# A linear recurrence feeding a soft mixture of experts: channel pairing, a fixed engine order, later weight loads and fewer exps

## The chip, the cores and the metric

The kernel runs on one core of a Trainium2 chip. The metric is the device time in microseconds (us) of one execution; where several executions were timed, I give the median. A core has TensorE (PE in the profile; PEld is its weight load), VectorE (DVE), ScalarE (ACT), GpSimd (POOL) and a queue engine (SP); data moves between memory and core by 16 DMA engines.

## The reference

Two stages. First, a gated recurrence along a sequence of 5056 tokens, for 4 batches and 256 channels. Then a soft mixture of 8 experts with 4 slots each over all 20224 tokens: a softmax over the tokens dispatches them to the slots, and a softmax over the 32 slots combines the answers.

```
sig = 1 / (1 + exp(-f_logit));  f = lb + (1 - lb) * sig;  i = 1 - f
for t in range(S):
    h = f[:, t] * h + i[:, t] * x[:, t]        # y[:, t] = h
logits = y @ phi                                # [20224, 32]
d = softmax over tokens(logits);  slot_input = d.T @ y
slot_out[e] = relu(slot_input[e] @ w1[e]) @ w2[e]
out = softmax over slots(logits) @ slot_out     # [20224, 256]
```

## The kernel before

The work is cut in *units*: 512 tokens of one batch (the last group has 448). There are 10 groups of 4 batches, so 40 units. A unit goes through these steps; this is the source, with cuts marked:

```python
W_FROM = 22            # a weight load at each of the units 22 to 37, as written
        def gate(n):
            n_p = rows(n // B)
            su = sup.tile([P, R, D, 2], BF16, name="su", tag="su")
            sus[n] = su
            nc.scalar.activation(su[:n_p, :, :, 1], fs.pop(n)[:n_p], ACT.Sigmoid,
                                 scale=-1.0)
            nc.gpsimd.tensor_tensor(su[:n_p, :, :, 0], su[:n_p, :, :, 1],
                                    xs.pop(n)[:n_p], ALU.mult)

        def to_channels(n):
            n_p = rows(n // B)
            su = sus.pop(n)
            for dc in range(DC):
                ps = psu.tile([P, P, R], F32, name="ps", tag="ps")
                for r in range(R):
                    nc.tensor.transpose(
                        ps[:, :n_p, r],
                        su[:n_p, r, ds(dc * P, P)].bitcast(F32).rearrange("p c o -> p (c o)"),
                        ident_f[:n_p, :n_p])
                pss[n, dc] = ps

        def scan(n):
            T = rows(n // B) * R
            h = hpool.tile([P, G, DC], BF16, name="h", tag="h")
            hs[n] = h
            for dc in range(DC):
                ps = pss.pop((n, dc)).rearrange("c p r -> c (p r)").bitcast(BF16)
                ps = ps.rearrange("c (t o) -> c t o", o=2)
                a = apool.tile([P, G], F32, name="a", tag="a")
                nc.scalar.activation(a[:, :T], ps[:, :T, 1], ACT.Identity,
                                     scale=nomlb[:, ds(dc, 1)], bias=1.0)
                nc.vector.tensor_tensor_scan(
                    h[:, :T, dc], a[:, :T], ps[:, :T, 0],
                    hs[n - B][:, ds(G - 1, 1), dc] if n >= B else 0.0,
                    ALU.mult, ALU.add)
        # ... to_tokens(n): 4 transposes of h back to tokens into hp, then a copy by DVE into ht
        # ... logits(g): 8 matmuls with phi for a group of 4 units, then exp by ACT into etall
        # ... weights_to_tokens(g): 4 transposes of etall into ep, copy into et, row sums into rsum (DVE)
        # ... slots(g): 16 matmuls, ht by et, summed over all tokens into slot_ps

        for n in range(n_unit + 8):
            if n + AHEAD < n_unit:
                load(n + AHEAD)
            if n + 2 < n_unit:
                gate(n + 2)
            if W_FROM <= n < W_FROM + 2 * E:
                load_w(n - W_FROM)
            if n + 1 < n_unit:
                to_channels(n + 1)
            if n < n_unit:
                scan(n)
            m = n - 1
            if 0 <= m < n_unit:
                to_tokens(m)
                if m % B == B - 1:
                    logits(m // B)
            m = n - 2
            if m >= 0 and m % B == B - 1 and m < n_unit:
                weights_to_tokens(m // B)
            m = n - 3
            if m >= 0 and m % B == B - 1 and m < n_unit:
                slots(m // B)
```

So ACT makes 1-sigmoid, POOL multiplies it with x, and both values of one channel lie side by side as two bf16 in one 32-bit word. PE transposes such words (as if they were f32) to channel-major, ACT turns one half into the decay `a` and DVE scans. **The order of instructions on an engine is not the order above**: a scheduler in the framework reorders them, and the trace shows in what order they ran.

After the recurrence comes a *middle* (normalisation and experts, mostly PE) and an *output* stage (a matmul per tile, scaling, and a store of 20.7 MB). The change leaves both as they are.

The softmax here doesn't subtract the row's maximum and nothing guards it: scores larger than these inputs give would overflow.

Of the kernel before, what the change touches and what calls it, by code (L numbers as in the profile page):

```python
# [18 lines left out]
def kernel(  # L19
# [19 lines left out]
    R = 4  # L39
# [10 lines left out]
    make_identity(nc, ident_f)  # L50
    ident = consts.tile([P, P], BF16, name="ident")
    nc.vector.tensor_copy(ident, ident_f)
# [9 lines left out]
    with nc.allow_non_contiguous_dma(reason="256 words"):  # L62
        nc.sync.dma_start(out=lb, in_=lower_bound.rearrange("(dc p) -> p dc", p=P))
# [5 lines left out]
    nc.sync.dma_start(out=phi_f, in_=moe_phi.rearrange("(dc p) s -> p dc s", p=P))  # L69
    phi = consts.tile([P, DC, NS], BF16, name="phi")  # L70
    for dc in range(DC):
        nc.vector.tensor_scalar_mul(phi[:, dc], phi_f[:, dc], omlb[:, ds(dc, 1)])
# [7 lines left out]
    csum = store.tile([P, n_grp], F32, name="csum")  # L80
    slot_sb = store.tile([P, D], F32, name="slot_sb")
    w1_r = moe_w1.rearrange("e (dc p) f -> e p dc f", p=P)
# [10 lines left out]
    W_FROM = 22  # L93

    with tc.tile_pool(name="ld", bufs=7) as ld, \
# [3 lines left out]
         tc.tile_pool(name="htok", bufs=2) as htok, \  # L99
         tc.tile_pool(name="etok", bufs=2) as etok, \  # L100
         tc.tile_pool(name="psu", bufs=4, space=PSUM) as psu, \
         tc.tile_pool(name="ptp", bufs=2, space=PSUM) as ptp, \
# [4 lines left out]
        xs, fs, sus, pss, hs, hps, hts, lgs, ets, eps = ({} for _ in range(10))  # L107
# [14 lines left out]
        def gate(n):  # L122
            n_p = rows(n // B)
            su = sup.tile([P, R, D, 2], BF16, name="su", tag="su")
            sus[n] = su
            nc.scalar.activation(su[:n_p, :, :, 1], fs.pop(n)[:n_p], ACT.Sigmoid,  # L126
                                 scale=-1.0)
            nc.gpsimd.tensor_tensor(su[:n_p, :, :, 0], su[:n_p, :, :, 1],  # L128
                                    xs.pop(n)[:n_p], ALU.mult)

        def to_channels(n):
            n_p = rows(n // B)
            su = sus.pop(n)
            for dc in range(DC):
                ps = psu.tile([P, P, R], F32, name="ps", tag="ps")
                for r in range(R):
                    nc.tensor.transpose(  # L137
                        ps[:, :n_p, r],
                        su[:n_p, r, ds(dc * P, P)].bitcast(F32).rearrange("p c o -> p (c o)"),
                        ident_f[:n_p, :n_p])  # L140
                pss[n, dc] = ps

        def scan(n):
            T = rows(n // B) * R
            h = hpool.tile([P, G, DC], BF16, name="h", tag="h")
            hs[n] = h
            for dc in range(DC):
                ps = pss.pop((n, dc)).rearrange("c p r -> c (p r)").bitcast(BF16)
                ps = ps.rearrange("c (t o) -> c t o", o=2)
                a = apool.tile([P, G], F32, name="a", tag="a")  # L150
                nc.scalar.activation(a[:, :T], ps[:, :T, 1], ACT.Identity,  # L151
                                     scale=nomlb[:, ds(dc, 1)], bias=1.0)
                nc.vector.tensor_tensor_scan(  # L153
                    h[:, :T, dc], a[:, :T], ps[:, :T, 0],
                    hs[n - B][:, ds(G - 1, 1), dc] if n >= B else 0.0,
                    ALU.mult, ALU.add)

        def to_tokens(n):
# [6 lines left out]
            if b == 0:  # L165
                hts[g] = htok.tile([P, B, R, D], BF16, name="ht", tag="ht")
            nc.vector.tensor_copy(  # L167
                hts[g][:n_p, b].rearrange("p r d -> p (r d)").bitcast(F32),
                hp[:n_p].rearrange("p r c -> p (r c)"))

        def logits(g):
            T = rows(g) * R
            lg = plg.tile([P, G], F32, name="lg", tag="lg")
            for dc in range(DC):
                for b in range(B):
                    nc.tensor.matmul(lg[ds(b * NS, NS), :T], phi[:, dc],  # L176
                                     hs[g * B + b][:, :T, dc],
                                     start=dc == 0, stop=dc == DC - 1,
                                     skip_group_check=True)
            nc.scalar.activation(etall[:, ds(g * G, T)], lg[:, :T], ACT.Exp,  # L180
                                 accum_out=csum[:, ds(g, 1)])
# [24 lines left out]
        AHEAD = 6  # L206
        for n in range(AHEAD):
            load(n)
        gate(0)
        gate(1)  # L210
        to_channels(0)
        for n in range(n_unit + 8):
            if n + AHEAD < n_unit:
                load(n + AHEAD)
            if n + 2 < n_unit:
                gate(n + 2)
            if W_FROM <= n < W_FROM + 2 * E:
                load_w(n - W_FROM)
            if n + 1 < n_unit:
                to_channels(n + 1)  # L220
            if n < n_unit:
                scan(n)
            m = n - 1
            if 0 <= m < n_unit:
                to_tokens(m)
                if m % B == B - 1:
                    logits(m // B)
            m = n - 2
            if m >= 0 and m % B == B - 1 and m < n_unit:
                weights_to_tokens(m // B)  # L230
# [112 lines left out]
```

## Time and profile before

The median is 277.25 us of 3 runs (277.19 to 278.37). The profiled execution spans 276.7 us.

| stretch of the profile (us) | what happens | us |
|---|---|---|
| 0 to 11.7 | first tokens land, first scan starts | 11.7 |
| 11.7 to 87.7 | units 0 to 12 are scanned | 76.0, 5.8 a unit |
| 87.7 to 193.7 | units 13 to 39 | 106.0, 3.9 a unit |
| 193.7 to 218.3 | middle | 24.6 |
| 218.3 to 276.7 | output | 58.4 |

From the page of the kernel before: the DVE row and the two DMA rows, for 40 equal slices of 6.9 us (a digit is tenths of busy time; GB/s is what was moved).

```profile
DVE  2386477365423959779596797958600375556450
DMA  6999999999999999978686840000000099999996
GB/s 184 415 309 300 305 301 304 301 276 278 277 278 391 410 410 409 397 261 286 219 322 195 260 135 0 0 0 2 0 2 0 2 383 405 404 405 405 403 381 213
```

The DMA engines are full in slices 2 to 17, yet move only some 300 GB/s in slices 3 to 12, while DVE is half idle. The missing bandwidth has a name in the timeline of POOL and in the list of DMA issues (last column: us from issue to landing). Two of the 16 weight loads, the first and the last, and the landing of the last:

```profile
9.68 0.89 POOL L89 DMA_DIRECT2D w_sb_90<-in_moe_w_dram  x1
55.49 0.59 POOL L91 DMA_DIRECT2D w_sb_105<-in_moe_w_dram  x1 [0.31 <-DMA w_sb_97<-in_moe_w_dram]
w_sb_105<-in_moe_w_dram POOLq DMA_DIRECT2D x1, 512.0 KB, 30.0
```

The source puts them at units 22 to 37; the scheduler has moved them up, and they share the DMA engines with the tokens until 85.5 us (55.5 + 30.0). They read 32-bit words and write bf16, so each counts 0.5 MB moved for 1 MB read (256 x 1024 words of 4 bytes), which is why "full" looks like 300 GB/s: 8.39 MB of weights in 76 us are 110 GB/s, and 301 + 110 is about the 410 of the slices without weights (an estimate). Their first use is at 199.5 us.

The table of stretches (busy us of each engine with its number of instructions, granted PE clock, DMA share, GB/s):

```profile
11.70:87.70 76.00, 43.51 (x250) 30.50 (x250) 42.46 (x46) 43.83 (x53) 41.68 (x30) 0.73 1.06 301
103.90:169.50 65.60, 45.26 (x312) 32.65 (x304) 52.25 (x57) 52.30 (x65) 37.49 (x17) 0.83 0.75 261
```

In the second stretch 16 units pass, 4.1 us each, with DMA to spare. DVE (third number, 52.25) and ACT (52.30) are busy 80% each: neither is full. The list of waits of the whole profile, cut to seven rows, says what waits for what (engine, its work, what released it: us in total, times, longest):

```profile
PE ps L137 <- POOL su L128: 52.1, 27, 9.8
POOL su L128 <- ACT su L126: 46.9, 21, 3.9
POOL su L128 <- DMA x_t<-in_x_dram: 32.2, 8, 5.9
DVE h L153 <- ACT a L151: 30.3, 14, 7.1
DVE ht L167 <- PE hp L164: 30.2, 16, 4.9
ACT a L151 <- PE ps L137: 29.5, 24, 4.9
ACT su L126 <- DMA f_t<-in_f_logit_dram: 24.2, 8, 4.6
```

The two DMA rows belong to the first stretch and the start before it (all but 2.8 us). The others form a ring: DVE waits for the decay, the decay for the transposes, those for POOL's product, that for the sigmoid. But the two stretches differ. DVE waits 26.4 of its 30.3 us for the decay in the first; between 103.9 and 169.5 us alone, the same list gives 28.2 us for POOL's wait for the sigmoid, 17.0 for PE's wait for the product, 11.0 for ACT's wait for the transposes, but for DVE only 1.3 us for the decay and 10.6 us for `hp`, the transposes of h back to tokens. In mid-recurrence DVE's idle time is 13.4 of 65.6 us. Last, three groups of instructions (count, busy us, mean ns, then idle time before them):

```profile
L128 POOL TENSOR_TENSOR su<-su,x_t 128x1024 bf16<-128x1024 bf16 x36 | 84.6, 2356 | 75.8 <-ACT su L126 39.7 <-DMA x_t<-in_x_dram 32.2 <-ACT a L151 2.6
L126 ACT ACTIVATE su<-f_t 128x1024 bf16<-128x1024 f32 x36 | 48.2, 1358 | 24.3 <-DMA f_t<-in_f_logit_dram 24.2
L126 ACT ACT_TABLE_LOAD x10 | 12.8, 1283 | 5.0 <-DMA f_t<-in_f_logit_dram 4.2 <-PEq L327 0.7
```

### The profile page before, as it was taken

To read this page: it belongs to the slowest core of one execution; us is meant where nothing else is said; L and a number is where in the kernel's file an instruction comes from. 1 tells how busy PE (TensorE), PEld (TensorE's weight loads), DVE (VectorE), ACT (ScalarE), POOL (GpSimd) and SP (SyncE) were. 2 spreads that over 40 slices of the span, in tenths; PEclk is the share of its full clock that TensorE was granted. 3 is DMA by queue.
4 is the path that set the end of the run, shared out by engine and by line. 5 is a ranking of instruction groups with operands and counts; after the bars stand their busy time and mean duration, and the time that the engine had idled before them with its cause. 6 is when DMAs were issued, how large, how long until landed. Compare 5 with 4: busy or idle time off the path is not lost. (4 is left out here: it accounts for less than half of the span.)

```text
span 276.7 us, 3255 instructions
## 1 busy us (share of the span) xinstructions
PE 175.5 (63%) x1118; PEld 119.2 (43%) x1118; DVE 163.4 (59%) x180; ACT 159.3 (58%) x232; POOL 111.9 (40%) x64
## 2 busy tenths in 40 slices
PE   0475755644564969566775866739599797677620
PEld 0344543423342746454553644526497532223310
DVE  2386477365423959779596797958600375556450
ACT  3577576553635596886869777795020255445440
POOL 1979746642225357365555746459300000000000
PEclk9999768765566666899798597995755955555555
DMA  6999999999999999978686840000000099999996
GB/s 184 415 309 300 305 301 304 301 276 278 277 278 391 410 410 409 397 261 286 219 322 195 260 135 0 0 0 2 0 2 0 2 383 405 404 405 405 403 381 213
DMA packets 20977, 70.77 MB, mean 256 GB/s; under 512 B 2720, under 2 KB 2720, under 8 KB 20960
## 3 DMA queue, kind: packets, MB, share of 16 engines
q1 hardware_dynamic: 17632, 62.17, 60.0%
q0 software_dynamic: 3328, 8.39, 15.5%
q8 instruction: 9, 0.15, 0.2%
q14 instruction: 8, 0.07, 0.1%
HBM read 58.23 MB, written 20.71 MB: 285 GB/s over the span
## 5 line engine op out<-in xcount | busy, mean ns | idle before, releaser
L128 POOL TENSOR_TENSOR su<-su,x_t 128x1024 bf16<-128x1024 bf16 (+1 forms) x40 | 93.9, 2356 | 83.1 <-ACT su L126 46.9
L153 DVE TENSOR_TENSOR_SCAN h<-a,h,ps 128x512 bf16<-128x512 f32 (+1 forms) x72 | 87.5, 1254 | 22.3 <-ACT a L151 21.8
L137 PE MATMUL ps<-ident_f,su 128*128 128x128 f32 (+1 forms) x320 | 59.8, 348 | 52.3 <-POOL su L128 52.1
L137 PEld LDWEIGHTS ps<-ident_f,su 128*128 128x128 f32 (+1 forms) x320 | 48.0, 181 | 66.6 <-POOL su L128 66.6
L151 ACT ACTIVATE a<-ps,nomlb 128x512 f32<-128x512 bf16 (+1 forms) x80 | 51.2, 673 | 31.9 <-PE ps L137 29.5
L126 ACT ACTIVATE su<-f_t 128x1024 bf16<-128x1024 f32 (+1 forms) x40 | 53.6, 1358 | 24.3 <-DMA f_t<-in_f_logit_dram 24.2
L308 ACT ACTIVATE ob<-op,rrow 128x256 f32<-128x256 f32 (+1 forms) x64 | 25.1, 474 | 35.0 <-PE op L296 12.1
L167 DVE COPY ht<-hp 128x512 f32<-128x512 f32 (+1 forms) x40 | 27.1, 678 | 30.3 <-PE hp L164 30.2
L296 PE MATMUL op<-slot_out,etall 32*128 32x256 bf16 (+1 forms) x160 | 34.2, 385 | 12.6 <-ACT ob L308 6.7
L164 PE MATMUL hp<-ident_f,h 128*128 128x128 f32 (+1 forms) x160 | 34.9, 352 | 9.4 <-DVE h L153 9.4
L302 DVE TENSOR_TENSOR ob<-op,rrow 128x1024 f32<-128x1024 f32 (+1 forms) x24 | 29.0, 1224 | 19.9 <-DMA out_dram<-ob 14.1
L164 PEld LDWEIGHTS hp<-ident_f,h 128*128 128x128 f32 (+1 forms) x160 | 26.7, 214 | 22.7 <-issue 18.1
L176 PE MATMUL lg<-h,phi 128*32 128x512 bf16 (+1 forms) x80 | 24.6, 471 | 9.7 <-DVE h L153 9.7
L296 PEld LDWEIGHTS <-etall 32*128 32x128 bf16 (+1 forms) x160 | 15.4, 130 | 31.2 <-issue 27.8
L126 ACT ACT_TABLE_LOAD x10 | 12.8, 1283 | 5.0 <-DMA f_t<-in_f_logit_dram 4.2
L153 DVE TENSOR_TENSOR_SCAN h<-a,ps 128x512 bf16<-128x512 f32 x8 | 9.4, 1213 | 8.5 <-ACT a L151 8.5
L180 ACT ACT_TABLE_LOAD x10 | 12.8, 1283 | 0.2
L284 DVE TENSOR_SCALAR slot_out<-so_ps,rcs 128x256 bf16<-128x256 f32 x1 | 0.5, 483 | 17.9 <-PE so_ps L279 17.9
L176 PEld LDWEIGHTS <-phi 128*32 128x32 bf16 x80 | 4.9, 96 | 11.5 <-issue 9.3
L200 PE MATMUL slot_ps<-ht,et 128*32 128x256 bf16 (+1 forms) x160 | 8.0, 332 | 2.9 <-DVE et L191 2.0
L272 ACT ACTIVATE hid<-h_ps 128x128 bf16<-128x128 f32 x8 | 2.2, 278 | 11.5 <-PE h_ps L268 11.5
L279 PEld LDWEIGHTS <-hid 128*128 128x128 bf16 x64 | 7.5, 122 | 2.0
(69 smaller groups left out, 88.7 us busy)
## 6 DMA issues: line engine op xcount, KB each, us to landing
f_t<-in_f_logit_dram SPq DMA_DIRECT2D x36, 512.0 KB, 10.2
x_t<-in_x_dram SPq DMA_DIRECT2D x36, 512.0 KB, 10.2
out_dram<-ob SPq DMA_DIRECT2D x36, 512.0 KB, 5.6
f_t<-in_f_logit_dram SPq DMA_DIRECT2D x4, 448.0 KB, 4.2
x_t<-in_x_dram SPq DMA_DIRECT2D x4, 448.0 KB, 4.0
out_dram<-ob SPq DMA_DIRECT2D x4, 448.0 KB, 5.9
w_sb_90<-in_moe_w_dram POOLq DMA_DIRECT2D x1, 512.0 KB, 10.4
w_sb_91<-in_moe_w_dram POOLq DMA_DIRECT2D x1, 512.0 KB, 12.1
```

Source lines behind the costliest of these rows:

```text
L126: nc.scalar.activation(su[:n_p, :, :, 1], fs.pop(n)[:n_p], ACT.Sigmoid, scale=-1.0)
L128: nc.gpsimd.tensor_tensor(su[:n_p, :, :, 0], su[:n_p, :, :, 1], xs.pop(n)[:n_p], ALU.mult)
L137: nc.tensor.transpose(ps[:, :n_p, r], su[:n_p, r, ds(dc * P, P)].bitcast(F32).rearrange("p c o -> p (c o)"), ident_f[:n_p, :n_p])
L151: nc.scalar.activation(a[:, :T], ps[:, :T, 1], ACT.Identity, scale=nomlb[:, ds(dc, 1)], bias=1.0)
L153: nc.vector.tensor_tensor_scan(h[:, :T, dc], a[:, :T], ps[:, :T, 0], hs[n - B][:, ds(G - 1, 1), dc] if n >= B else 0.0, ALU.mult, ALU.add)
L164: nc.tensor.transpose(hp[:n_p, r], hw[:, :n_p, r], ident_f)
L167: nc.vector.tensor_copy(hts[g][:n_p, b].rearrange("p r d -> p (r d)").bitcast(F32), hp[:n_p].rearrange("p r c -> p (r c)"))
L176: nc.tensor.matmul(lg[ds(b * NS, NS), :T], phi[:, dc], hs[g * B + b][:, :T, dc], start=dc == 0, stop=dc == DC - 1, skip_group_check=True)
L180: nc.scalar.activation(etall[:, ds(g * G, T)], lg[:, :T], ACT.Exp, accum_out=csum[:, ds(g, 1)])
L296: nc.tensor.matmul(op[:n_p, r], ew[ds(b * NS, NS), :, r], slot_out[ds(b * NS, NS), :], start=True, stop=True, skip_group_check=True)
L302: nc.vector.tensor_tensor(ob[:n_p], op[:n_p], rrow[:n_p, g, :, ds(b, 1)].broadcast_to([n_p, R, D]), ALU.mult)
L308: nc.scalar.activation(ob[:n_p, r], op[:n_p, r], ACT.Copy, scale=rrow[:n_p, g, r, ds(b, 1)])
```

## The change

Its intent, in four parts:

1. **Words of neighbouring channels.** 1-sigmoid and the product get tiles of their own, and a word now holds two neighbouring channels of one quantity. The transposes of 1-sigmoid (`sp`) no longer depend on POOL's product (`up`).
2. **Fixed order.** The recurrence is issued in the order written.
3. **Paced weight loads.** Five loads between units 4 and 28, the other eleven from unit 33, when the token loads are nearly all issued.
4. **exp for two groups at once**, since a switch between sigmoid and exp costs two table loads on ACT. One `ht` copy in four also moves from DVE to ACT.

```diff
+    word = consts.tile([P, P, 2], BF16, name="word")      # identity, by way of two transposes
+    # ... memset, copy, PE transpose, ACT copy, PE transpose, DVE copy
     ident = consts.tile([P, P], BF16, name="ident")
-    nc.vector.tensor_copy(ident, ident_f)
+        nc.vector.tensor_copy(ident, word_t[:, :, 0])
-        nc.sync.dma_start(out=lb, ...)                    # and phi_f: on the SP queue
+    nc.scalar.dma_start(out=lb, ...)                      # and phi_f: on the ACT queue
-    W_FROM = 22
+    W_AT = {4: 1, 10: 1, 16: 1, 22: 1, 28: 1, 33: 1, 34: 2, 35: 2, 36: 2, 37: 2, 38: 2}
         # buffers: ld 7 -> 6, htok 2 -> 4, etok 2 -> 3; PSUM: psu 4 -> 2 of each kind, ptp 2 -> 1, lg twice as wide
         def gate(n):
-            su = sup.tile([P, R, D, 2], BF16, ...)        # both values of a channel in one word
+            sts[n] = sup.tile([P, R, D], BF16, name="s_t", tag="s_t")
+            uts[n] = sup.tile([P, R, D], BF16, name="u_t", tag="u_t")
         # to_channels: 4 transposes of s_t into sp, then 4 of u_t into up
-            nc.vector.tensor_copy(hts[g]...)
+            copy = nc.scalar.copy if b == 1 else nc.vector.tensor_copy
+        def batch_of(g):
+            return [g & ~1, g | 1] if g < n_grp - 2 else [g]
+        with tc.manual_schedule():
+            # ...
+            for n in range(n_unit + 6):
+                # load(n + 5)
+                # decay(n)
+                m = n - 2
+                if m >= 0 and m % B == B - 1 and m < n_unit:
+                    exps(m // B)                          # at the second group of a pair
+                # to_channels(n + 1)
+                # gate(n + 2)
+                # weight loads of W_AT
+                # scan(n)
+                # to_tokens(n - 1), and logits of a finished group
+                # weights_to_tokens and slots, of the two groups of a pair in consecutive units
```

More of the change, by code (lines that the diff above doesn't have):

```diff
@@ L50 @@
     make_identity(nc, ident_f)
+    word = consts.tile([P, P, 2], BF16, name="word")
+    nc.vector.memset(word.rearrange("p c o -> p (c o)"), 0.0)
+    nc.vector.tensor_copy(word[:, :, 0], ident_f)
+    word_t = consts.tile([P, P, 2], BF16, name="word_t")
     ident = consts.tile([P, P], BF16, name="ident")
-    nc.vector.tensor_copy(ident, ident_f)
+    with tc.tile_pool(name="psi", bufs=1, space=PSUM) as psi:
+        ip = psi.tile([P, P], F32, name="ip")
+        iw = psi.tile([P, P], F32, name="iw")
+        w_f = word.bitcast(F32).rearrange("p c o -> p (c o)")
+        wt_f = word_t.bitcast(F32).rearrange("p c o -> p (c o)")
+        nc.tensor.transpose(ip, w_f, ident_f)
+        nc.scalar.copy(wt_f, ip)
+        nc.tensor.transpose(iw, wt_f, ident_f)
+        nc.vector.tensor_copy(wt_f, iw)
+        nc.vector.tensor_copy(ident, word_t[:, :, 0])
     rep = consts.tile([P, B, NS], F32, name="rep")
@@ L61 @@
     lb = consts.tile([P, DC], F32, name="lb")
-    with nc.allow_non_contiguous_dma(reason="256 words"):
-        nc.sync.dma_start(out=lb, in_=lower_bound.rearrange("(dc p) -> p dc", p=P))
+    nc.scalar.dma_start(out=lb, in_=lower_bound.rearrange("(p o) -> p o", o=DC))
     omlb = consts.tile([P, DC], F32, name="omlb")
@@ L68 @@
     phi_f = consts.tile([P, DC, NS], F32, name="phi_f")
-    nc.sync.dma_start(out=phi_f, in_=moe_phi.rearrange("(dc p) s -> p dc s", p=P))
+    nc.scalar.dma_start(out=phi_f, in_=moe_phi.rearrange("(p o) s -> p o s", o=DC))
     phi = consts.tile([P, DC, NS], BF16, name="phi")
-    for dc in range(DC):
-        nc.vector.tensor_scalar_mul(phi[:, dc], phi_f[:, dc], omlb[:, ds(dc, 1)])
+    for o in range(DC):
+        nc.vector.tensor_scalar_mul(phi[:, o], phi_f[:, o], omlb[:, ds(o, 1)])
     store = ctx.enter_context(tc.tile_pool(name="store", bufs=1))
@@ L80 @@
     csum = store.tile([P, n_grp], F32, name="csum")
+    nc.vector.memset(csum, 0.0)
     slot_sb = store.tile([P, D], F32, name="slot_sb")
-    w1_r = moe_w1.rearrange("e (dc p) f -> e p dc f", p=P)
+    w1_r = moe_w1.rearrange("e (p o) f -> e p o f", o=DC)
     w2_r = moe_w2.rearrange("e (p fc) d -> e p fc d", p=P)
@@ L91, in load_w @@
             nc.gpsimd.dma_start(out=w2_sb[i - E], in_=w2_r[i - E])
-    W_FROM = 22
-    with tc.tile_pool(name="ld", bufs=7) as ld, \
+    W_AT = {4: 1, 10: 1, 16: 1, 22: 1, 28: 1, 33: 1, 34: 2, 35: 2, 36: 2, 37: 2, 38: 2}
+    w_next = [0]
+    with tc.tile_pool(name="ld", bufs=6) as ld, \
          tc.tile_pool(name="sup", bufs=3) as sup, \
@@ L98 @@
          tc.tile_pool(name="hpool", bufs=9) as hpool, \
-         tc.tile_pool(name="htok", bufs=2) as htok, \
-         tc.tile_pool(name="etok", bufs=2) as etok, \
-         tc.tile_pool(name="psu", bufs=4, space=PSUM) as psu, \
-         tc.tile_pool(name="ptp", bufs=2, space=PSUM) as ptp, \
+         tc.tile_pool(name="htok", bufs=4) as htok, \
+         tc.tile_pool(name="etok", bufs=3) as etok, \
+         tc.tile_pool(name="psu", bufs=2, space=PSUM) as psu, \
+         tc.tile_pool(name="ptp", bufs=1, space=PSUM) as ptp, \
          tc.tile_pool(name="plg", bufs=1, space=PSUM) as plg, \
@@ L106 @@
         slot_ps = pslot.tile([P, D], F32, name="slot_ps")
-        xs, fs, sus, pss, hs, hps, hts, lgs, ets, eps = ({} for _ in range(10))
+        xs, fs, sts, uts, pss, psus, hs, hps, hts, lgs, ets = ({} for _ in range(11))
         def load(n):
@@ L123, in gate, with decay @@
             n_p = rows(n // B)
-            su = sup.tile([P, R, D, 2], BF16, name="su", tag="su")
-            sus[n] = su
-            nc.scalar.activation(su[:n_p, :, :, 1], fs.pop(n)[:n_p], ACT.Sigmoid,
-                                 scale=-1.0)
-            nc.gpsimd.tensor_tensor(su[:n_p, :, :, 0], su[:n_p, :, :, 1],
-                                    xs.pop(n)[:n_p], ALU.mult)
+            sts[n] = sup.tile([P, R, D], BF16, name="s_t", tag="s_t")
+            nc.scalar.activation(sts[n][:n_p], fs.pop(n)[:n_p], ACT.Sigmoid, scale=-1.0)
+            uts[n] = sup.tile([P, R, D], BF16, name="u_t", tag="u_t")
+            nc.gpsimd.tensor_tensor(uts[n][:n_p], sts[n][:n_p], xs.pop(n)[:n_p], ALU.mult)
         def to_channels(n):
             n_p = rows(n // B)
-            su = sus.pop(n)
-            for dc in range(DC):
-                ps = psu.tile([P, P, R], F32, name="ps", tag="ps")
+            for src, dst, tag in ((sts, pss, "sp"), (uts, psus, "up")):
+                t = src.pop(n).bitcast(F32)
+                ps = psu.tile([P, P, R], F32, name=tag, tag=tag)
                 for r in range(R):
-                    nc.tensor.transpose(
-                        ps[:, :n_p, r],
-                        su[:n_p, r, ds(dc * P, P)].bitcast(F32).rearrange("p c o -> p (c o)"),
-                        ident_f[:n_p, :n_p])
-                pss[n, dc] = ps
+                    nc.tensor.transpose(ps[:, :n_p, r], t[:n_p, r], ident_f[:n_p, :n_p])
+                ps = ps.rearrange("c p r -> c (p r)").bitcast(BF16)
+                dst[n] = ps.rearrange("c (t o) -> c t o", o=DC)
+        decays = {}
+        def decay(n):
+            T = rows(n // B) * R
+            sp = pss.pop(n)
+            for o in range(DC):
+                a = apool.tile([P, G], F32, name="a", tag="a")
+                nc.scalar.activation(a[:, :T], sp[:, :T, o], ACT.Identity,
+                                     scale=nomlb[:, ds(o, 1)], bias=1.0)
+                decays[n, o] = a
         def scan(n):
@@ L146, in scan @@
             hs[n] = h
-            for dc in range(DC):
-                ps = pss.pop((n, dc)).rearrange("c p r -> c (p r)").bitcast(BF16)
-                ps = ps.rearrange("c (t o) -> c t o", o=2)
-                a = apool.tile([P, G], F32, name="a", tag="a")
-                nc.scalar.activation(a[:, :T], ps[:, :T, 1], ACT.Identity,
-                                     scale=nomlb[:, ds(dc, 1)], bias=1.0)
+            up = psus.pop(n)
+            for o in range(DC):
                 nc.vector.tensor_tensor_scan(
-                    h[:, :T, dc], a[:, :T], ps[:, :T, 0],
-                    hs[n - B][:, ds(G - 1, 1), dc] if n >= B else 0.0,
+                    h[:, :T, o], decays.pop((n, o))[:, :T], up[:, :T, o],
+                    hs[n - B][:, ds(G - 1, 1), o] if n >= B else 0.0,
                     ALU.mult, ALU.add)
@@ L166, in to_tokens, with exps @@
                 hts[g] = htok.tile([P, B, R, D], BF16, name="ht", tag="ht")
-            nc.vector.tensor_copy(
-                hts[g][:n_p, b].rearrange("p r d -> p (r d)").bitcast(F32),
-                hp[:n_p].rearrange("p r c -> p (r c)"))
+            copy = nc.scalar.copy if b == 1 else nc.vector.tensor_copy
+            copy(hts[g][:n_p, b].rearrange("p r d -> p (r d)").bitcast(F32),
+                 hp[:n_p].rearrange("p r c -> p (r c)"))
+        def batch_of(g):
+            return [g & ~1, g | 1] if g < n_grp - 2 else [g]
         def logits(g):
             T = rows(g) * R
-            lg = plg.tile([P, G], F32, name="lg", tag="lg")
-            for dc in range(DC):
+            gs = batch_of(g)
+            if g == gs[0]:
+                lgs[0] = plg.tile([P, 2 * G], F32, name="lg", tag="lg")
+            lg = lgs[0][:, ds((g - gs[0]) * G, T)]
+            for o in range(DC):
                 for b in range(B):
-                    nc.tensor.matmul(lg[ds(b * NS, NS), :T], phi[:, dc],
-                                     hs[g * B + b][:, :T, dc],
-                                     start=dc == 0, stop=dc == DC - 1,
+                    nc.tensor.matmul(lg[ds(b * NS, NS), :], phi[:, o],
+                                     hs[g * B + b][:, :T, o],
+                                     start=o == 0, stop=o == DC - 1,
                                      skip_group_check=True)
-            nc.scalar.activation(etall[:, ds(g * G, T)], lg[:, :T], ACT.Exp,
-                                 accum_out=csum[:, ds(g, 1)])
+        def exps(g):
+            gs = batch_of(g)
+            if g == gs[-1]:
+                T = sum(rows(i) for i in gs) * R
+                nc.scalar.activation(etall[:, ds(gs[0] * G, T)], lgs[0][:, :T], ACT.Exp,
+                                     accum_out=csum[:, ds(g, 1)])
         def weights_to_tokens(g):
@@ L204, in slots @@
                                      skip_group_check=True)
-        AHEAD = 6
-        for n in range(AHEAD):
-            load(n)
-        gate(0)
-        gate(1)
-        to_channels(0)
-        for n in range(n_unit + 8):
-            if n + AHEAD < n_unit:
-                load(n + AHEAD)
-            if n + 2 < n_unit:
-                gate(n + 2)
-            if W_FROM <= n < W_FROM + 2 * E:
-                load_w(n - W_FROM)
-            if n + 1 < n_unit:
-                to_channels(n + 1)
-            if n < n_unit:
-                scan(n)
-            m = n - 1
-            if 0 <= m < n_unit:
-                to_tokens(m)
-                if m % B == B - 1:
-                    logits(m // B)
-            m = n - 2
-            if m >= 0 and m % B == B - 1 and m < n_unit:
-                weights_to_tokens(m // B)
-            m = n - 3
-            if m >= 0 and m % B == B - 1 and m < n_unit:
-                slots(m // B)
+        AHEAD = 5
+        with tc.manual_schedule():
+            for n in range(AHEAD):
+                load(n)
+            gate(0)
+            to_channels(0)
+            gate(1)
+            for n in range(n_unit + 6):
+                if n + AHEAD < n_unit:
+                    load(n + AHEAD)
+                if n < n_unit:
+                    decay(n)
+                m = n - 2
+                if m >= 0 and m % B == B - 1 and m < n_unit:
+                    exps(m // B)
+                if n + 1 < n_unit:
+                    to_channels(n + 1)
+                if n + 2 < n_unit:
+                    gate(n + 2)
+                for _ in range(W_AT.get(n, 0)):
+                    load_w(w_next[0])
+                    w_next[0] += 1
+                if n < n_unit:
+                    scan(n)
+                m = n - 1
+                if 0 <= m < n_unit:
+                    to_tokens(m)
+                    if m % B == B - 1:
+                        logits(m // B)
+                for lag, step in ((3, weights_to_tokens), (4, slots)):
+                    for i in range(2):
+                        m = n - lag - i
+                        if m >= 0 and m % B == B - 1 and m < n_unit:
+                            gs = batch_of(m // B)
+                            if m // B == gs[-1] and i < len(gs):
+                                step(gs[i])
         nc.vector.tensor_copy(slot_sb, slot_ps)
@@ L254 @@
         sin_ps = eps1.tile([P, DC, NS], F32, name="sin_ps")
-        slot_v = slot_sb.rearrange("p (c dc) -> p dc c", dc=DC)
+        slot_v = slot_sb.rearrange("p (c o) -> p o c", o=DC)
         for dc in range(DC):
```

## The prediction

> **What bounds the kernel now.** The span (276.7 us) has three parts: recurrence, to 193.7 us (last scan in the timeline of DVE); middle (experts), to 218.3 us, where the chain of waits is an almost unbroken line of PE work; output, to 276.7 us at about 405 GB/s, DMA bound. The change alters only the first part, of 40 units:
> - 11.7 (first scan) to 87.7 us: only 13 units, 5.8 us each. The timeline of POOL shows all 16 weight loads issued from 9.7 to 55.5 us, long before they are needed; the last takes 30 us to land. The table of stretches shows DMA share 1.06, and SP issues a pair of token loads every 5.3, later 7.5 us; with the weights gone, 2.6 us. ACT and POOL wait 24 and 32 us for f_t and x_t, almost all here. The Trainium skill, "Trainium Kernel Development and Optimization", Key Constraints, says that all issuing queues run on the same 16 DMA engines and interleave; the trace agrees.
> - 103.9 to 169.5 us: 16 units, 4.1 us each, DMA share 0.75. DVE and ACT are both busy 52.3 of 65.6 us: order and latency bind, not one full engine. ACT waits for ps, POOL for ACT, PE for POOL; two sigmoids run in a row behind exp.
>
> **What the change does.**
> 1. Weight pacing: 5 loads spread over units 4 to 28, 11 from unit 33, when the last token loads are out. Tokens at 410 GB/s need 2.6 us a unit and no longer limit. The largest part: the first 13 units fall from 5.8 us to the compute pace, about 27 us saved.
> 2. exp for two groups: 6 exps instead of 10. Each costs two table loads of 1.283 us (the skill, "ScalarE: Activation LUTs", What ACT_TABLE_LOAD costs, gives 1283 ns plus a drain; in the trace exp starts right after the load, so I count no drain). Saves about 10 us of ACT, 0.26 us a unit.
> 3. Fixed order: no double sigmoids; PE's transposes of sigma needn't wait for POOL's product, so the decay is ready early.
> 4. Neighbouring channels in a word: same transposes, scans (1.25 us) and POOL product (2.36 us; I expect no gain). One ht copy in four moves from DVE to ACT.
>
> Pace, estimated from start-to-start times: DVE 2x1.2 + 0.75x0.65 + 0.27 = 3.2 us a unit; ACT 1.29 + 1.24 + 0.15 + 3.7/8 = 3.15; POOL 2.4; PE 2.2 at full clock, 3.7 at half. Added stalls: per eight units, exp holds ACT 3.6 us and the ACT copy waits for PE (about 3 us together); ep and hp share one buffer, 0.65 us a group. So 3.65 us a unit. Scans end near 11 + 40x3.65 - 1 = 156 us instead of 193.7. The 83 us after the last scan stay: 239 us of span.
>
> **Prediction: 240 us, 8 in 10 between 230 and 250.** Faster by over 2%: 0.97; within 2%: 0.02; slower: 0.01.
>
> **What would show it.** Step 1: ACT's wait for f_t falls from 24 to under 6 us; units scanned by 88 us rise from 13 to over 20. Step 2: 6 exps, 12 or 13 table loads. Step 3: PE's wait for POOL's product falls from 52 to under 25 us; DVE over 85% busy in mid-recurrence. Step 4: POOL 2.36 us, scan 1.25. Output 58 us, middle 24 to 26.
>
> **What would make it wrong.** A fixed order that makes one engine wait in every unit (ACT for PE, PE cold at half clock): 4 us a unit gives 253. The late 11 weights delaying the experts: POOL must issue them by 145 us. If order hides all stalls, 3.3 us a unit gives 226.

## The result, and the profile after

The new kernel takes 241.34 us (median of 4 runs, 240.37 to 242.37) against 277.33 us for the one before on the same chip. The ratio is 0.870 (95% interval 0.864 to 0.875). Ratios here are the mean time of one kernel's fast runs over that of the other's of the same rounds, so not quite the ratio of the medians quoted.

The same rows of the page of the new kernel (240.4 us, slices of 6.0 us):

```profile
DVE  0967999569994999859998588651005766455530
DMA  6999999999999889998996799991001999999996
GB/s 225 414 411 408 411 333 410 410 362 377 414 356 307 282 267 318 330 346 279 253 274 168 127 187 210 204 213 22 3 0 53 404 405 406 404 406 402 408 354 214
```

The slow region of slices 3 to 12 is gone: some 410 GB/s are moved from slice 2 on (333 in one slice), and the weights fill slices 22 to 27, with half the words counted as above. The stretches: the first units, the middle of the recurrence and the output.

```profile
13.80:44.50 30.70, 21.24 (x136) 17.02 (x134) 27.78 (x28) 25.98 (x37) 20.38 (x11) 0.94 1.03 396
44.50:130.80 86.30, 55.38 (x456) 44.34 (x456) 74.08 (x78) 65.97 (x91) 53.21 (x29) 0.86 0.96 319
182.60:240.40 57.80, 34.68 (x160) 15.55 (x159) 29.03 (x25) 25.06 (x64) 0.00 (x0) 0.52 0.93 359
```

From 44.5 to 130.8 us, 24 units pass: 3.6 us each. DVE is busy 86% (74.08 of 86.3), up from 80%. The last scan ends at 156.2 us instead of 193.7; the middle takes 26.4 us (24.6 before), the output 57.8 (58.4). The waits:

```profile
POOL u_t L143 <- ACT s_t L141: 41.4, 16, 4.3
ACT ht L187 <- PE hp L183: 20.1, 10, 2.7
PE up L151 <- POOL u_t L143: 18.5, 13, 1.6
ACT a L162 <- PE sp L151: 15.9, 9, 3.4
DVE et L222 <- PE ep L219: 14.8, 10, 2.5
POOL u_t L143 <- DMA x_t<-in_x_dram: 8.6, 3, 4.8
DVE h L172 <- ACT a L162: 6.0, 6, 1.3
DVE ht L187 <- PE hp L183: 2.5, 3, 1.2
ACT s_t L141 <- DMA f_t<-in_f_logit_dram: 3.5, 2, 1.8
```

The waits for tokens are nearly gone, DVE's wait for the decay has fallen from 30.3 to 6.0 us, and its wait for `hp` from 30.2 to 2.5. Two rows are new: ACT waits for `hp` (the copy it took over from DVE), and DVE for `ep`, the transposes of the exp weights to tokens. The three groups:

```profile
L143 POOL TENSOR_TENSOR u_t<-s_t,x_t 128x1024 bf16<-128x1024 bf16 x36 | 76.8, 2148 | 51.4 <-ACT s_t L141 36.0 <-DMA x_t<-in_x_dram 8.6 <-PE hp L183 5.9
L141 ACT ACTIVATE s_t<-f_t 128x1024 bf16<-128x1024 f32 x36 | 38.4, 1066 | 3.5 <-DMA f_t<-in_f_logit_dram 3.5
L141 ACT ACT_TABLE_LOAD x6 | 7.7, 1283 | 1.8 <-PEq L366 1.7
```

The sigmoid takes 1066 ns instead of 1358, and POOL's product 2148 instead of 2356: both now write adjacent bf16 elements, where they wrote every second one. I had not foreseen the first.

### The profile page after: what moved, and what is told of

Its sections match the earlier page's. It is cut to its first block, busy times and chain, and to the rows that moved or that the text cites. A ratio compares the mean times of both kernels' runs of the same rounds, so it can differ in the third digit from the quotient of the medians.

```text
span 240.4 us, 3205 instructions
## 1 busy us (share of the span) xinstructions
PE 153.8 (64%) x1120; PEld 110.2 (46%) x1120; DVE 160.1 (67%) x174; ACT 140.0 (58%) x227; POOL 101.8 (42%) x64
## 5 line engine op out<-in xcount | busy, mean ns | idle before, releaser
L143 POOL TENSOR_TENSOR u_t<-s_t,x_t 128x1024 bf16<-128x1024 bf16 (+1 forms) x40 | 85.4, 2149 | 56.9 <-ACT s_t L141 41.4
L172 DVE TENSOR_TENSOR_SCAN h<-a,h,up 128x512 bf16<-128x512 f32 (+1 forms) x72 | 86.7, 1251 | 5.5 <-ACT a L162 5.5
L162 ACT ACTIVATE a<-sp,nomlb 128x512 f32<-128x512 bf16 (+1 forms) x80 | 50.4, 688 | 15.9 <-PE sp L151 15.9
L151 PE MATMUL up<-ident_f,u_t 128*128 128x128 f32 (+1 forms) x160 | 31.3, 329 | 25.4 <-POOL u_t L143 18.5
L347 ACT ACTIVATE ob<-op,rrow 128x256 f32<-128x256 f32 (+1 forms) x64 | 25.1, 474 | 34.9 <-DVE ob L341 14.1
L141 ACT ACTIVATE s_t<-f_t 128x1024 bf16<-128x1024 f32 (+1 forms) x40 | 42.6, 1065 | 3.5 <-DMA f_t<-in_f_logit_dram 3.5
L151 PE MATMUL sp<-ident_f,s_t 128*128 128x128 f32 (+1 forms) x160 | 31.0, 327 | 13.5 <-ACT s_t L141 11.8
L151 PEld LDWEIGHTS up<-ident_f,u_t 128*128 128x128 f32 (+1 forms) x160 | 22.5, 171 | 31.0 <-POOL u_t L143 26.7
L151 PEld LDWEIGHTS sp<-ident_f,s_t 128*128 128x128 f32 (+1 forms) x160 | 21.5, 167 | 20.5 <-ACT s_t L141 13.9
L335 PEld LDWEIGHTS <-etall 32*128 32x128 bf16 (+1 forms) x160 | 15.7, 131 | 31.1 <-issue 27.6
L187 DVE COPY ht<-hp 128x512 f32<-128x512 f32 (+1 forms) x30 | 20.2, 672 | 2.6 <-PE hp L183 2.5
L187 ACT COPY ht<-hp 128x512 f32<-128x512 f32 (+1 forms) x10 | 5.9, 585 | 20.1 <-PE hp L183 20.1
L222 DVE COPY et<-ep 128x512 bf16<-128x512 bf16 (+1 forms) x10 | 4.2, 425 | 14.8 <-PE ep L219 14.8
L219 PE MATMUL ep<-ident,etall 128*128 128x128 bf16 (+1 forms) x40 | 5.4, 278 | 11.5 <-DVE ht L187 7.4
L172 DVE TENSOR_TENSOR_SCAN h<-a,up 128x512 bf16<-128x512 f32 x8 | 9.2, 1206 | 2.4 <-PE up L151 1.9
```

What stands on the lines that cost most here:

```text
L141: nc.scalar.activation(sts[n][:n_p], fs.pop(n)[:n_p], ACT.Sigmoid, scale=-1.0)
L143: nc.gpsimd.tensor_tensor(uts[n][:n_p], sts[n][:n_p], xs.pop(n)[:n_p], ALU.mult)
L151: nc.tensor.transpose(ps[:, :n_p, r], t[:n_p, r], ident_f[:n_p, :n_p])
L162: nc.scalar.activation(a[:, :T], sp[:, :T, o], ACT.Identity, scale=nomlb[:, ds(o, 1)], bias=1.0)
L172: nc.vector.tensor_tensor_scan(h[:, :T, o], decays.pop((n, o))[:, :T], up[:, :T, o], hs[n - B][:, ds(G - 1, 1), o] if n >= B else 0.0, ALU ...
L187: copy(hts[g][:n_p, b].rearrange("p r d -> p (r d)").bitcast(F32), hp[:n_p].rearrange("p r c -> p (r c)"))
```

## The experiments

Twelve kernels were run, all correct. All comparisons are of fast runs, save that two of the four runs of e10, the profiled one among them, were slow (over 1.5% above its fastest); its ratio leaves them out. The new kernel itself was timed only in the first call; later runs are set against its 241.34 us across calls. The median of before lay between 277.2 and 278.0 us. A pace is worked out as the time between the starts of two scans, over the units between them.

### Pacing, undone and alone (e1, e2)

My theory (A): weight loads starved the first units. The rival (B): pacing is incidental, the order gained.

e1, on the new kernel:

```diff
-    W_AT = {4: 1, 10: 1, 16: 1, 22: 1, 28: 1, 33: 1, 34: 2, 35: 2, 36: 2, 37: 2, 38: 2}
+    W_AT = {0: 2, 1: 2, 2: 1, 3: 2, 4: 2, 5: 1, 6: 1, 7: 2, 8: 2, 9: 1}
```

> The kernel after, with one thing undone: the 16 weight loads go out during units 0 to 9, as they did in the kernel before, instead of units 4 to 38. Theory A (the shared DMA engines starved the first units): the first stretch falls back to about 5 us or more a unit until some 80 us, ScalarE and POOL wait for f_t and x_t again 20 us or more each, and the time is 241 plus 20 to 28 us, 261 to 269 us. Rival B (the fixed order is what gained, and pacing is incidental because the later units catch up): less than 8 us lost, under 249 us.

Measured: 268.92 us (268.29 to 270.75), 27.6 us more than the new kernel. The stretch of the first 15 units, and two of its waits:

```profile
13.80:91.20 77.40, 42.38 (x247) 32.14 (x246) 44.49 (x45) 38.45 (x54) 40.79 (x31) 0.68 1.05 308
ACT s_t L141 <- DMA f_t<-in_f_logit_dram: 33.4, 10, 5.3
POOL u_t L143 <- DMA x_t<-in_x_dram: 33.2, 9, 5.4
```

That is 5.2 us a unit (77.4 / 15) with the DMA engines full; later, from 94.1 us, 16 units take 58.9 us, 3.7 each, nearly as in the new kernel. Theory A holds in size and place.

e2, on the kernel before: a load now has to wait for a unit.

```diff
+        nc.gpsimd.tensor_copy(first, after)     # one element of the weight tile <- the unit's product
         nc.gpsimd.dma_start(out=w1_sb[i], in_=w1_r[i])
```

> The kernel before, with one thing added: each weight load waits for the gate product of a unit (a one-element copy on POOL that the load then overwrites), at the units of the kernel after (4 to 38). Theory A: the first 13 units fall from 5.8 to the kernel's own later pace of 4.1 us a unit, which saves 13 x 1.7 = 22 us: 255 us, and no more, since 4.1 us a unit is set by order and latency. Rival B: under 8 us saved, above 269 us.

Measured: 261.59 us (260.58 to 261.91), ratio 0.942. It saves 16 us, not 22. ACT's wait for f_t falls from 24.2 to 5.0 us, so the starvation is gone, and 16 units in mid-recurrence take 66.0 us, 4.12 each, as expected. The missing part lies at the start: the first five units take 25.3 us, 5.1 each, with no wait for tokens in them (the longest there are POOL's for the sigmoid, 11.0 us, and DVE's for the decay, 10.8, of which 6.8 lie before the first scan). So the first 13 take 58.2 us, not 13 x 4.1 = 53, and the other 27 take 107.3, against 106.0 before. The old order was slow in the first units by itself, apart from the weights.

So pacing is worth 16 us under the old order and 27.6 us under the new one. The rest of the change together is worth 277.7 to 268.9 (8.8 us) with starved units, and 20 us (261.59 to 241.34) without; the next run asks how much of that is the order. A faster pace can't be used while the tokens are late.

### The order, undone (e4)

e4 lets the scheduler order the recurrence of the new kernel; the weights are held back as in e2.

```diff
-        with tc.manual_schedule():
+        with ExitStack():
```

> The kernel after with the fixed order taken away (the scheduler orders the instructions of the recurrence), but the weight loads held to the same units by a one-element copy on POOL. Words of neighbouring channels, exp pairs, copies on ScalarE stay. Theory: the order itself is worth what is left of the change from 4.1 to 3.6 us a unit after exp pairs and the shorter sigmoid: 250 us, between 245 and 256. Rival: the fixed order is worth nothing beside pacing and exp pairs: 239 to 244 us.

Measured: 261.97 us (261.47 to 262.88): 20.6 us lost, more than I expected, and the same as e2 (261.59), which has none of the new layout, exp pairs and ACT copies. **Without the order the other edits bring nothing measurable; with them in place, the order is worth about 20 us.** Two limits: e4 keeps the buffers that were chosen for the fixed order (one for `hp` and `ep`, where e2 has two) and the new start (first scan at 13.9 us, 11.5 in e2), so a scheduler with the old ones might do somewhat better. And no run undoes the new layout or the ACT copy alone under the fixed order, so what they add there is not shown. The pace in mid-recurrence is 4.27 us (16 units in 68.3). Three of its waits (the longest of all is POOL's for the sigmoid, 65.2 us):

```profile
ACT a L167 <- PE sp L156: 50.7, 36, 3.1
DVE h L177 <- PE up L156: 27.1, 21, 3.0
PE lg L207 <- DVE h L177: 22.7, 23, 1.6
```

The first row is the one to read: the decay waits 50.7 us for transposes. In units 10 to 33 it starts 0.04 us after `sp` every time, while in the new kernel `sp` is done 1.7 us ahead of it on average. The sigmoid itself was done 1.1 us before `sp` starts, on average (0.2 to 2.4). The third suggests why here: matmuls of the logits stand in PE's queue ahead of them, and wait for the scan in progress. In e2 that third row is only 2.0 us, and there PE waits 52.6 us for POOL's product instead; so two different bad orders give nearly the same pace.

### One bad place in the order, on purpose (e5)

e5 keeps the fixed order, and puts the logits of each unit where the scheduler liked them: both halves, each behind a part of the unit's own scan. (Single exps make room in PSUM; e3 below shows that they cost nothing here.)

```diff
                 if n < n_unit:
+                    scan(n)
+                    logits(n, 0)            # first half, ahead of the transposes of unit n + 1
                 # to_channels(n + 1), gate(n + 2), to_tokens(n - 1)
+                    logits(n, 1)            # instead of all logits of a group at its end
```

> The kernel after with the fixed order kept, exp once per group (which the run before showed to cost nothing), and the logits matmuls of each unit placed where the scheduler of the kernel before puts them: the first half right behind the first half of the scan, ahead of the transposes of the next unit. Theory A (what the fixed order gained is that no matmul on PE waits for the scan in progress ahead of the transposes that feed the next decay): the chain half scan 1.25, logits 0.4, transposes 0.65 to 1.1, decay 0.7 us takes about 3.3 to 3.6 us a unit, longer than DVE's own 3.2, so the pace falls back to 3.9 to 4.2 us a unit and the time to 252 to 262 us. Rival B (the gain lies in ScalarE's order, sigmoid and exp): under 246 us.

Measured: 297.37 us (296.73 to 297.98), slower than the kernel before (ratio 1.073). The direction is that of theory A, the size is twice and more what I expected: 5.0 us a unit (24 units in 120.5 us). Two of its waits and one unit of its timeline (the longest wait of all is POOL's for the sigmoid, 99.1 us):

```profile
PE lg L199 <- DVE h L172: 69.1, 40, 2.6
ACT a L162 <- PE sp L151: 48.9, 21, 3.4
104.58 0.39 PE L199 MATMUL lg<-h,phi 128*32 128x512 bf16 x1 [2.50 <-DVE h L172]
104.90 0.66 PE L151 MATMUL sp<-ident_f,s_t 128*128 128x128 f32 x4
106.89 0.58 ACT L187 COPY ht<-hp 128x512 f32<-128x512 f32 x1 [2.16 <-PE hp L183]
107.37 1.27 ACT L162 ACTIVATE a<-sp,nomlb 128x512 f32<-128x512 bf16 x2
```

PE sits 2.5 us idle behind the logits, whose scan began at 103.25, before it may transpose data that was ready (that sigmoid ended at 102.6). Then ACT's queue does the same again: `sp` is done at 105.6, but the decay starts at 107.4, because the `ht` copy ahead of it waits for PE. I had counted only the first. The Trainium skill ("TensorE: Matmul & The Clock Gate", Part 3, The mechanism) says that matmuls start and end in strict order, without reordering; this trace agrees: the 2.5 us above are spent ahead of ready work, and waits of this kind come to 69.1 us. What e5 does not show is that logits alone made the old pace: the kernel before had 9.7 us of this wait, e4 22.7, e2 2.0.

### exp pairs, undone (e3)

```diff
-            return [g & ~1, g | 1] if g < n_grp - 2 else [g]
+            return [g]
```

> The kernel after with exp taken once for every group (10 exps, 20 table loads) instead of once per two groups. The prediction's term was 0.26 us a unit, so about 10 us in all if ScalarE's time is on the path: 249 to 252 us. Rival: ScalarE is not the bound (busy 22 of 28.9 us per eight units), so the four more exps cost only part of their 2.8 us plus 0.4 us each: under 246 us.

Measured: 241.22 us (240.32 to 241.94), against 241.34: no difference, where the prediction had put 10 us. The ten exps and twenty table loads are in the trace again, but ACT has the time. The pace in the profiles is 3.65 us against 3.60, at most 2 us over all units (from first scan to last 143.2 us against 142.3). **The pairs take 10 us off an engine, and nothing off the kernel.**

### The start (e6)

Between the two profiles the first scan had moved the wrong way, from 11.7 to 13.8 us. From the timeline of the new kernel, then two lines of e3, whose start is the same program:

```profile
4.96 0.17 DVE L78 TENSOR_SCALAR omlb<-lb 128x2 f32<-128x2 f32 x1 [3.94 <-DMA lb<-in_lower_bound_dram]
6.28 2.13 POOL L143 TENSOR_TENSOR u_t<-s_t,x_t 128x1024 bf16<-128x1024 bf16 x1 [4.84 <-DMA x_t<-in_x_dram]
6.42 2.18 DVE L85 TENSOR_SCALAR phi<-phi_f,omlb 128x32 bf16<-128x32 f32 x2 [1.22 <-DMA phi_f<-in_moe_phi_dram]
8.65 2.75 DVE L71 COPY rep<-ident_f 32x128 f32<-32x128 f32 x4
8.87 2.21 POOL L143 TENSOR_TENSOR u_t<-s_t,x_t 128x1024 bf16<-128x1024 bf16 x1 [0.46 <-DMA x_t<-in_x_dram]
```

```profile
5.40 0.39 DVE L85 TENSOR_SCALAR phi<-phi_f,omlb 128x32 bf16<-128x32 f32 x2 [1.23 <-DMA phi_f<-in_moe_phi_dram]
5.83 2.75 DVE L71 COPY rep<-ident_f 32x128 f32<-32x128 f32 x4
```

The lower bound, on another queue, lands after the first tokens. DVE's small setup then coincides with POOL's products and is stretched: 2.18 us for two operations and 2.75 for four, which took 0.39 and 0.90 us in the kernel before. PE waits behind it for the identity and starts its first transposes at 11.8 us. In e3 the lower bound landed 1.0 us earlier: its `phi` ran before POOL's first product (at 6.10 us) and took 0.39 us, its `rep` ran during it and took 2.75, and the first scan came at 11.5 us. e7 starts in the same way, e1, e4, e5 and e8 late like the new kernel. So in the profiles the start of this program varies by some 2.4 us; the new kernel's own runs lie 2.0 us apart (240.37 to 242.37). e6 restores the old setup:

```diff
-    nc.scalar.dma_start(out=lb, ...)   # and phi_f
+    nc.sync.dma_start(out=lb, ...)     # ahead of the tokens
-    # the identity by two transposes
+    nc.vector.tensor_copy(ident, ident_f)
```

> The kernel after with the constants of the kernel before: lower bound and phi loaded on the SP queue ahead of the tokens, identity by one cast. Theory: the first scan, at 13.8 us in the profile of after against 11.7 before and 11.5 in another run, comes at 11 to 11.7 us in every run, and the time is 239 us, with less spread. Rival: the start is hidden by what follows: 241 us.

Measured: 239.21 us (239.04 to 239.95), 2.1 us less and with less spread, as expected. The first scan starts at 10.5 us, the two groups take 0.39 and 0.90 us again, done by 5.1 us, before POOL begins. The Trainium skill ("GPSIMD Engine Reference", 1. Specifications) says that POOL shares its SBUF interfaces with VectorE and that some DVE instructions contend with it; the trace agrees with that reading (676 ns for a copy that takes 216), and `phi` in e3 against the new kernel shows it in the same program (0.39 us before POOL begins, 2.18 during its product). e6 itself changed the queue and the identity together, so it doesn't say which of the two gained.

### Two holes in the new order (e7, e8)

The new waits, ACT for `hp` and POOL for `s_t`, come from two places in the order. e7 puts the transposes of h between those of `sp` and `up`; e8 puts the sigmoid in front of exp.

```diff
 # e7, on PE                              # e8, on ACT
-  to_channels(n + 1): sp, up             -  decay(n), exps(n - 2), gate(n + 2)
-  ... to_tokens(n - 1): hp               +  decay(n), gate(n + 2), exps(n - 2)
+  sp(n + 1), hp(n - 1), up(n + 1)
```

> The kernel after with one order changed on PE: the transposes of h to tokens come between those of sigma and those of the product, so that they no longer wait for POOL. Theory: ScalarE's wait for hp (20.1 us in after) falls under 8 us, the wait of DVE for ep (14.8 us) falls too, the pace from 3.6 to about 3.4 us a unit: 233 to 237 us. Rival: those waits are slack, DVE is held by something else: 239 to 243 us.

Measured: 232.52 us (230.19 to 233.13), 8.8 us less. ACT's wait for `hp` falls from 20.1 to 3.8 us, DVE's for `ep` from 14.8 to 6.0. The theory holds, though part may be the start, which was early in the profiled run (230.19 us, first scan at 11.5). Of e7, and then of e8 below:

```profile
ACT ht L195 <- PE hp L185: 3.8, 5, 1.9
ACT ht L187 <- PE hp L183: 7.4, 6, 2.2
```

> The kernel after with the sigmoid of two units ahead placed before the exp of the pair instead of behind it. Theory: POOL's product is no longer 3.6 us late once per eight units, POOL's wait for s_t (41.4 us) falls by about 10 us, and the time by 2 to 5 us: 236 to 239 us. Rival: exp then delays the decay of the next unit instead, same time, 240 to 243 us.

Measured: 229.0 us (227.16 to 229.85), 12.3 us less, where I had expected 2 to 5. POOL's wait for `s_t` falls by only 5.7 us (41.4 to 35.7), but ACT's for `hp` falls from 20.1 to 7.4. The reason fits e7: with exp first, the sigmoid is 3.7 us late (table load, exp and table load, 96.71 to 100.43 us in the timeline of the new kernel), so the product is, so `up` is, and `hp` stands behind `up` in PE's queue. e7 takes `hp` out of that chain; e8 takes the delay out. e8 also has two table loads fewer (10 against 12), since no sigmoid follows the exp of the last group but one; what that is worth was not separated.

### The holes together, and single exps (e9, e10, e11, e12)

e9 has the edits of e6, e7 and e8.

> The three edits of the last call together on the kernel after: old start, transposes of h before those of the product, sigmoid before exp. Theory: they close different holes in part of DVE's idle time (the old start 2 us, the other two 8.8 and 12.3 us, which overlap, since both make the product's lateness harmless). DVE itself needs 3.16 us a unit, so the floor is 10.5 + 40 x 3.16 + 83 = 220 us: 221 to 226 us. If the two were independent: 218 us. Rival: they close the same hole: 226 to 229 us.

Measured: 227.28 us (226.01 to 228.06): hardly better than e8 alone. Singly they had saved 2.1 + 8.8 + 12.3 = 23.2 us, together 14.1: e7 and e8 close the same hole, as the rival had it.

e10 is e9 with one exp per group.

> The run before it in this call, with exp once per group again. It asks whether exp pairs are worth something once the holes behind exp are closed. If ScalarE's time were on the path, 4 more exps of 3.2 us less 0.5 us would cost 10 us. Theory: DVE is the limit, ScalarE has 2.9 + 0.5 or 0.8 us a unit against DVE's 3.16, so that single exps put ScalarE at 3.5 us a unit where it had slack: 3 to 8 us longer. Rival: still no difference (under 2 us), the pairs never paid.

Measured: 221.68 us (median of 4, 218.53 to 223.2; two of these slow), ratio of the fast runs to before 0.791 (0.785 to 0.797). Both theories were wrong: **single exps are not dearer, they are cheaper**, by 5.6 us between the medians (4.3 between the profiled runs, though e10's was a slow one; e12 below repeats it with six fast runs). For 24 units in mid-recurrence, e9 and then e10:

```profile
46.36:125.85 79.49, 55.81 (x458) 44.01 (x457) 73.73 (x80) 65.49 (x91) 53.69 (x30) 0.84 1.03 347
45.91:122.33 76.42, 56.31 (x459) 43.16 (x457) 73.68 (x79) 73.75 (x103) 53.73 (x30) 0.88 1.04 358
```

ACT gets 8.3 us more work, DVE the same, and the units take 3.1 us less: DVE is busy 96% instead of 93%. In these stretches DVE waits 5.6 us for `ep` in e9 and 2.4 in e10, a difference as large as that in time. My reading, not tested: with pairs, the `ep` steps of two groups fall in consecutive units, and each stands in PE's queue until the copy that frees the one PSUM buffer of `hp` and `ep`.

e11 moves a second `ht` copy in four to ACT (on top of e9), and the reciprocal of the row sums behind the copy of the slots.

```diff
-            copy = nc.scalar.copy if b == 1 else nc.vector.tensor_copy
+            copy = nc.scalar.copy if b % 2 else nc.vector.tensor_copy
```

> The three edits, and the ht copies of two batches in four (not one) on ScalarE, and the reciprocal of the row sums behind the copy of the slots instead of before it. DVE falls to 3.0 us a unit and ScalarE rises to about 3.05; the tail loses 1.15 us. Theory: 3 to 6 us below the run with three edits if DVE is the limit. Rival: ScalarE's waits for PE come back and it is no faster.

Measured: 230.27 us (229.02 to 230.83), 3 us slower than e9. The rival holds: ACT waits 21.6 us for `hp` again.

e12 is e10 with two PSUM buffers for `hp` and `ep`; the single exps leave a bank free.

```diff
-         tc.tile_pool(name="ptp", bufs=1, space=PSUM) as ptp, \
+         tc.tile_pool(name="ptp", bufs=2, space=PSUM) as ptp, \
-                lgs[0] = plg.tile([P, 2 * G], F32, name="lg", tag="lg")
+                lgs[0] = plg.tile([P, G], F32, name="lg", tag="lg")
```

> The kernel of the last call with three edits and single exps (221.7 us), with the bank of PSUM that the single exps leave free given to the tile shared by hp and ep (two buffers instead of one). Theory: what made pairs cost time is that the transposes of the exp weights (ep) wait in PE's order for the copy that frees the one buffer, and with two groups in consecutive units twice as closely; with two buffers PE's wait for the ht copies (hp 20, ep 10 us there) falls under 8 us in all, DVE's wait for ep (6.7 us) under 3, and the time by 1 to 4 us: 217 to 221 us. Rival: DVE is already at its floor, no change, 221 to 222 us.

Measured: 221.45 us (220.5 to 222.18, six fast runs), ratio 0.799 (0.796 to 0.801). No gain over e10, within the spread. DVE's wait for `ep` falls from 6.7 to 1.3 us, yet DVE was near its floor: 73.95 us busy in 76.6 for 24 units. So the buffer is not what limits e10. Whether it is what made the *pairs* dear stays open: no run has pairs with two buffers.

e10 and e12 beat both kernels: at about 221.5 us they take 20% less time than the kernel before, and 8% less than the new one (241.34). Their recurrence differs from the new kernel by this:

```diff
+  constants as in the kernel before (e6)
+  PE: sp(n + 1), hp(n - 1), up(n + 1) (e7);  ACT: decay(n), gate(n + 2), exps(n - 2) (e8)
+  exp once per group (e3);  e12 also: ptp 1 -> 2 buffers, lg one bank
```

## Why the prediction was right or wrong

The total was right: 240 predicted, 241.34 measured. That is in part luck: two of its parts were off in opposite directions, by 10 and some 12 us.

- **What bounds the kernel: right.** Starved first units (e1, e2), then order and latency (e4). DVE and ACT at 80% were not the limit, though e10 and e12 end with DVE at 96%.
- **Step 1, pacing, 27 us: right.** Undone in the new kernel it costs 27.6 us. ACT's wait for f_t fell to 3.5 us (predicted under 6); 21 units were scanned by 88 us (predicted over 20). Alone on the old order it brings only 16 us, which the prediction did not claim.
- **Step 2, exp pairs, 0.26 us a unit: wrong.** The 6 exps and 12 table loads are there and ACT is relieved, but e3 puts the worth at 0 to 2 us, and e10 shows it negative once the other holes are closed. The prediction itself said that no engine was full, and then counted the busy time of one as time saved.
- **Step 3, fixed order: right in kind, too small.** I gave it no figure of its own; of the fall from 4.1 to 3.65 us a unit, I had put 0.26 on the exps, which leaves 0.2 a unit, 8 us. e4 puts it at 20.6 us. PE's wait for the product fell to 18.5 us (predicted under 25) and DVE reached 86% (predicted over 85). The reason given, that the decay is ready early, is only part of it: in mid-recurrence the kernel before lost only 1.3 us of DVE to the decay, but 10.6 to `hp`. Also, DVE's own work fell from 3.27 to 3.09 us a unit there (52.25 / 16, 74.08 / 24), about the 0.67 us copy in four that went to ACT; the prediction counted that, and no run isolates it.
- **Step 4, the layout: partly wrong.** The scan stayed (1.25 us); POOL's product fell to 2.15 us (I expected no gain) and the sigmoid to 1.07. In e4 neither shows in the time.
- **The pace, 3.65 us: right at 3.60**, with the stalls where I put them: exp holding ACT, the ACT copy waiting for PE, and `ep` and `hp` sharing a buffer. e7 and e8 show that these were the price of the order as written: without them the pace is 3.4, and 3.2 in e10.
- **The ends: two small misses that the sum hid.** The first scan came at 13.8 us, not 11 (e6: 2.1 us); the 83 us after the last scan became 84.2, of which the middle 26.4 (I said 24 to 26).
- **What would make it wrong** did not come: the late weights were issued by 152 us, 7 us later than I had allowed, and the experts did not wait for them.

## What to carry to other kernels

A queue that runs in order stands behind its slowest head: place an instruction that must wait (a copy of a fresh result, a matmul on a running scan) behind the work that feeds the next round. Here the logits in a bad place cost 56 us (e5), and the sigmoid in a better one saved 12 (e8). Before counting a saving, ask whether the engine it relieves is full; the exp pairs took 10 us off ScalarE, and gave nothing, later less than nothing. Load what is needed last, last, even where the queue looks free: the same 16 loads cost 16 us under a slow pace and 27.6 us under a fast one.

## What the Trainium skill lacked or had wrong

- "ScalarE: Activation LUTs", What ACT_TABLE_LOAD costs: the 1283 ns of a table load are met exactly. The page adds about 1380 ns of drain to every switch; here, with the engine never idle, a load starts 0.02 us after the decay before it (96.71 after 96.69) and exp starts at 98.01, so a switch costs 1.3 us in all.
- The same page and section give 186 ns + 0.833 ns an element for an instruction with immediate scale and bias, an estimate of 1039 ns at 1024 elements. The sigmoid takes 1066 ns when it writes adjacent bf16, but 1358 ns when it writes every second one; the page has no term for the stride of the output.
- "GPSIMD Engine Reference", 7. Performance pitfalls for Q7 kernels, lists a penalty for bf16 reads only at steps above 4 elements. POOL's product already falls from 2356 to 2148 ns when one input and the output go from a step of 2 to adjacent elements; which of the two did it was not separated.
